# A windowed-attention and Fourier-mixing stack: logits and probabilities kept as heads, rows, keys; channel-matrix splits and cell sums moved among the second tile's steps

## The chip, the cores and the metric

The kernel runs on one core of one Trainium2 chip. A core has TensorE (PE in the profile; PEld is its weight load), VectorE (DVE), ScalarE (ACT), GpSimd (POOL) and SyncE (SP, which here issues nearly all transfers), and sixteen DMA engines between its on-chip memory (SBUF) and HBM. PE writes its results to a second on-chip memory, PSUM, in eight banks. The metric is the device time of one execution in microseconds, as a median over executions. Less is better.

## The reference

Four layers act on x of 2048 positions by 640 channels: attention, Fourier mixing, attention, Fourier mixing. Each adds its result to its input, and each normalises its input first.

```python
def _A_ref(x, wqkv, wo):            # H = 32 heads of Dh = 20, window W = 8, dilation 2
    q, k, v = ...                   # x @ wqkv
    idx = pos[:, None] - off[None, :]       # positions s, s-2, ..., s-14
    logits = jnp.einsum("bhsd,bhswd->bhsw", q, kg) * scale
    logits = jnp.where(mask, logits, -1e9)
    attn = _softmax(logits, axis=-1)
    o = jnp.einsum("bhsw,bhswd->bhsd", attn, vg)
    return o.reshape(B, S, D) @ wo
...
def _B_ref(x, dft_seq_re, dft_seq_im, dft_hid_re, dft_hid_im):
    a = jnp.einsum("bsd,ed->bse", x, dft_hid_re)
    b = jnp.einsum("bsd,ed->bse", x, dft_hid_im)
    return jnp.einsum("ts,bse->bte", dft_seq_re, a) - jnp.einsum("ts,bse->bte", dft_seq_im, b)
...
x = A_x
x = x + _A_ref(_layernorm(x), A_wqkv, A_wo)
x = x + _B_ref(_layernorm(x), ...)
x = x + _A_ref(_layernorm(x), A_wqkv, A_wo)
x = x + _B_ref(_layernorm(x), ...)
```

So every position attends to eight keys in each head, and each Fourier layer is a real part of a two-dimensional transform written as products with given matrices.

## The kernel before

**Precision and data.** Matrices are multiplied in a reduced format, so each factor is split into a high and a low part: ACT writes the high part, DVE (or POOL) subtracts it from the source and writes the low part, and PE makes three products (`PASSES`, L215). Positions are permuted on the host, even ones first, so that the dilated window becomes eight neighbouring rows. A chunk `c` is 512 positions: 128 partitions of four rows `j`.

**Attention (`layer_a`, L239).** A plan of steps is written out by hand: `at(step, phase, fn)` records work, and the loop at L816 replays it in the order of steps and, in a step, of `PHASES` (L808), so the order on all five engines is fixed (L812). A unit `u` is one chunk and four heads (`HE`), in two halves `jp` of two rows; unit u has steps 2u and 2u+1, and there are 32 units a layer. For a half:

- `qk_mul` (L425) multiplies queries by the keys' window on DVE into `pr`, as rows, keys, heads, channels; POOL adds the ten upper channels of each head to the ten lower ones (L430).
- `qk_red` (L433) sums the ten remaining channels on DVE into the logits `lg`, 64 results for a half. `lg` is laid out as rows, keys, heads: `[P, NJ, W, HE]`.
- `soft` (L446) acts on a whole unit, 128 logits a partition: the mask (L451), the maximum over keys (L453), its subtraction (L455), the sum (L457) after ACT's exponential, the reciprocal (L459), and the product (L461), which writes the probabilities to a bank of PSUM that stays allocated (`pq`). `mx` and `sm`, 16 values each, lie in the same bank as rows, heads.
- `av_mul` (L464) multiplies the window of values by each probability, repeated over 20 channels; POOL adds the eight keys in three instructions (`av_tree`, L474).

The products with the weights (L359), with the output matrix (L506) and, late in the layer, the first output tile of the next Fourier layer (`z_mm`, L907) are put between these steps.

**Fourier mixing (`LayerB`, L845).** The sequence transform comes first, for eight tiles of 256 output positions: a tile is 16 steps over the 2048 input positions, and a step is fifteen matmuls into five banks (`z_mm`). The result is copied and split out of the banks (`evac`, L980, through `zt_put`, L960) and multiplied with the channel matrices (`ymm`, L985), whose result is added to the layer's input and stored (`yout`, L1004; the additions are L1009). Tiles 0 and 1 are made so; the other six go in three pairs by a scheme with seven products in place of eight (`pair`, L1093), which needs sums and differences of blocks of the input (cells): `x_whole` (L1036) adds high and low parts, `x_combine` (L1043) makes one combination (L1049), splits it in a buffer `stg` of which there are two (L1050, L1051), and stores it to HBM (L1052). `load_w` (L926) loads and splits the two channel matrices, five pieces each, through a ring of two buffers `xa`; the splits are L128 on ACT, L132 and L130 on DVE.

`run` (L1229) puts this together: the evacuation of tile 0, all of `load_w`, then sixteen steps of tile 1, with the first output block's `ymm` and `yout` behind step 3, two fifths of the second block's `ymm` behind step 13, and three items of cell work behind each step from step 2 on. In `run` only PE's order is fixed by hand (L1236); the order on the other engines comes from the compiler's own scheduler. All of them work in order, SP's queue of transfers too.

Of the kernel before, what the change touches and what calls it, by code (L numbers as in the profile page):

```python
# [36 lines left out]
LEAD0 = (-7, -6, -5, -4, -3, -2, -1, 0, 1, 1, 2, 3, 3, 4, 5, 5)  # L37


THIN = ((20, 24, 26, 28, 32, 36, 40, 44), (12, 16, 20, 24, 28, 32, 36, 44, 48))  # L40
OUTP = (((20, 24, 28, 32), (36, 40, 44, 46)), ((20, 24, 28, 32), (36, 40, 44, 46)))
LNS = ((40, 52), (40, 52))


LEAD2 = (-7, -6, -5, -4, -2, 0, 0, 1, 1, 2, 3, 4, 4, 6, 6, 7)
ZTHIRDS = (
# [4 lines left out]
)  # L51
# [3 lines left out]
NWIN = 5  # L55
# [19 lines left out]
def tile_layers(ctx: ExitStack, tc: tile.TileContext, x, wqkv, wo, cs, wre, wim, out):  # L75
# [21 lines left out]
    nc.vector.memset(warm, 0.0)  # L97
    nc.scalar.activation(warm, warm, AF.Exp)
    T([P, 8], "pad0")
# [34 lines left out]
    class Stats:  # L134
        def __init__(self):
# [30 lines left out]
        def var_eps(self, j):  # L166
            nc.scalar.activation(self.rstd[:, j : j + 1], self.var[:, j : j + 1], AF.Copy, bias=EPS, scale=1.0 / D)  # L167

        def finish(self, j0=0, j1=4):
            r = self.rstd[:, j0:j1]  # L170
# [19 lines left out]
    def load_x(src, j, tag="xa"):  # L190
        xt = T([P, D], tag, bufs={"xa": 2}.get(tag, 1))
# [47 lines left out]
    def layer_a(li, stats, handoff, prev):  # L239
        xin, xout = xs[li], xs[li + 1]  # L240
        first = li == 0
        ly = li // 2
        nstats = [None] * NC
# [7 lines left out]
        win = {}  # L251
        lgs = {}
# [18 lines left out]
        def x_stats(c, j, fast=False):  # L271
            if j == 0:
                stats[c] = Stats()
# [88 lines left out]
        def qkv_evac(g, cqj):  # L362
            c, q, j = cqj
            if j % 2 == 0:
                sgs[q] = T([P, 6, 2, FE], "stg", bufs=2)
# [21 lines left out]
        def q_load(u):  # L387
            c, e = u // NE, half(u, 0)[0]
            src = qb[c][e // 2]
            qs[u] = T([P, NJ, FE], "qs")  # L390
# [34 lines left out]
        def qk_mul(u, jp):  # L425
# [4 lines left out]
            nc.gpsimd.tensor_tensor(pv[:, :, 0:10], pv[:, :, 0:10], pv[:, :, 10:20], op=ALU.add)  # L430
            prq[(u, jp)] = pv

        def qk_red(u, jp):  # L433
            if jp == 0:
                lgs[u] = T([P, NJ, W, HE], "lg", bufs=2)
            nc.vector.tensor_reduce(  # L436
                lgs[u][:, 2 * jp : 2 * jp + 2].rearrange("p j w h -> p (j w h)"),
                prq.pop((u, jp))[:, :, 0:10],
# [7 lines left out]
        def soft(u, part):  # L446
            lg = lgs[u]
            v = nc.vector
            if part == 0 and (u // NE) % 2 == 0:
                mw = bass.AP(tensor=mk.tensor, offset=mk.offset, ap=[mk.ap[0], [1, NJ], [1, W], [0, HE]])  # L450
                v.tensor_tensor(lg, lg, mw, op=ALU.add)  # L451
            if part == 1:
                v.tensor_reduce(mx, lg.rearrange("p j w h -> p j h w"), axis=AX.X, op=ALU.max)  # L453
            if part == 2:
                v.tensor_tensor(lg, lg, mx.unsqueeze(2).to_broadcast([P, NJ, W, HE]), op=ALU.subtract)  # L455
            if part == 3:
                v.tensor_reduce(sm, lg.rearrange("p j w h -> p j h w"), axis=AX.X, op=ALU.add)  # L457
            if part == 4:
                v.reciprocal(sm, sm)  # L459
            if part == 5:  # L460
                v.tensor_tensor(pp, lg, sm.unsqueeze(2).to_broadcast([P, NJ, W, HE]), op=ALU.mult)  # L461
                lgs[u] = pp

        def av_mul(u, jp):  # L464
            pr = prod()
            nc.vector.tensor_tensor(  # L466
                pr.rearrange("p j w (h d) -> p j w h d", d=DH),
                lgs[u][:, 2 * jp : 2 * jp + 2].unsqueeze(4).to_broadcast([P, 2, W, HE, DH]),
                wview(u, jp, 1, [[DH, HE], [1, DH]]),
# [44 lines left out]
        def wo_add(c, j, e0=0, e1=2):  # L514
            for e in range(e0, e1):
                if e == 0 and j == 0:
                    nstats[c] = Stats()
# [27 lines left out]
        def wq_split(q, k):  # L545
            split(wq[q][:, 0, k], wq[q][:, 1, k], wq[(q, k)], eng=nc.gpsimd if k % 2 else None)
# [23 lines left out]
        def early():  # L570
# [8 lines left out]
            def xt(j, part):  # L579
# [3 lines left out]

            prev.pair(
                NPAIR - 1,
                stats,
                {
# [731 lines left out]
```

## Time and profile before

| | before |
|---|---|
| median of three runs | 1804.51 us |
| lowest, highest | 1800.17, 1807.22 us |
| the profiled execution | 1801.87 us |
| span of its instructions | 1800.0 us |
| mean granted PE clock | 0.991 |
| first attention layer | up to about 400 us |
| second attention layer | about 930 to 1290 us |
| DMA, moved | 423.59 MB, mean 235 GB/s |

A profile is of one execution, and its busy times are shares of an average over stages with different limits. A group of instructions is given by source line, engine, operation, the tiles written and read, and shapes, with busy time, mean nanoseconds of one, and what ended the idle time ahead of it. The chain of waits is followed back from the last instruction, at each step to what released it; a piece of another engine in it says that this engine's time passes on to the end. A filter by stretch gives each engine's busy microseconds and, in brackets, its instructions.

### The profile page before, as it was taken

Reading aid. Unit: us, or ns where it says so; the run is one execution under the profiler, and the core shown is the slowest. Engines: PE = TensorE matmul, PEld = TensorE weight load, DVE = VectorE, ACT = ScalarE, POOL = GpSimd, SP = SyncE. Lnnn points to the kernel's source line nnn. Section 1 sums busy time; section 2 is a strip of 40 time slices with the busy share of each in tenths; the row PEclk is TensorE's granted clock in tenths of the full one; section 3 lists DMA queues with packets and bytes.
Section 4 is the critical chain, followed back from the end, with each engine's and each line's share of the span. In section 5 each row is a group of like instructions: output and inputs, shape, how many; then the busy total and the mean of one; then the engine's idle time right before and its main releaser. Section 6 shows DMA issues by size and latency. Waiting matters only on the chain.

```text
span 1800.0 us, 26493 instructions
## 1 busy us (share of the span) xinstructions
PE 1735.3 (96%) x8798; PEld 1506.4 (84%) x8798; DVE 1391.0 (77%) x2135; ACT 818.6 (45%) x1708; POOL 633.5 (35%) x591
## 2 busy tenths in 40 slices
PE   9999997989999999999999999998899999999999
PEld 6889896877788888888888899987787888888888
DVE  5899899987767767768739988899777676677673
ACT  5544644544445445445533334444434443443441
POOL 3799898960000000000008987889400000000000
PEclk9999999999999999999999999999999999999999
DMA  6776667648787887888737856687687876876861
GB/s 232 225 264 205 212 206 250 216 147 293 255 264 256 284 271 251 290 270 268 246 124 223 284 183 199 201 300 260 218 283 258 265 237 219 267 230 228 265 211 53
DMA packets 273994, 423.59 MB, mean 235 GB/s; under 512 B 22688, under 2 KB 153248, under 8 KB 273600
## 3 DMA queue, kind: packets, MB, share of 16 engines
q1 hardware_dynamic: 270656, 419.92, 71.7%
q10 hardware_dynamic: 3200, 1.97, 0.4%
q8 instruction: 70, 1.15, 0.3%
q14 instruction: 68, 0.56, 0.1%
HBM read 336.66 MB, written 85.14 MB: 234 GB/s over the span
## 4 chain that ended last, share of the span: by engine, by line
PE 63%; DVE 14%; DMA 11%; POOL 6%; ACT 3%; issue 2%; SPq 0%; DVEq 0%; ACTq 0%; POOLq 0%
PE m L359 16%; PE aux L996 12%; PE t L1085 9%; PE m L1085 9%; PE pq L1085 5%; PE xt L1085 4%; DMA xc<-stg 4%; PE aux L506 4%; DVE pr L428 2%; DMA win<-cs_in 2%; DVE pr L466 2%; POOL pr L481 2%; POOL pr L430 1%; POOL r L868 1%; DMA xa<-cs_in 1%
## 5 line engine op out<-in xcount | busy, mean ns | idle before, releaser
L359 PE MATMUL m<-r,s 128*128 128x480 f32 x1920 | 438.9, 383 | 6.2 <-ACT s L229 3.8
L359 PEld LDWEIGHTS m<-r,s 128*128 128x128 f32 x1920 | 358.1, 190 | 60.8 <-ACT s L229 5.5
L1078 ACT CAST r<-win 128x512 fp32r<-128x512 f32 x251 | 152.9, 620 | 175.3 <-DVE win L1114 86.9
L171 POOL TENSOR_TENSOR stats<-stats,mhalf 128x1 f32<-128x1 f32 (+1 forms) x40 | 29.1, 727 | 565.8 <-ACT stats L167 565.7
L996 PE MATMUL aux<-r2a,zo 128*128 128x320 f32 x768 | 226.0, 309 | 0.0
L481 POOL TENSOR_TENSOR pr<-pr 128x640 f32<-128x640 f32 x126 | 204.5, 1623 | 41.9 <-DVE pr L466 41.5
L428 DVE TENSOR_TENSOR pr<-pq,win 128x1280 f32<-128x1280 f32 x128 | 189.8, 1483 | 26.9 <-ACT pq L401 24.6
L996 PE MATMUL aux<-pr,zo 128*128 128x320 f32 x704 | 207.8, 309 | 0.0
L1079 DVE TENSOR_TENSOR r<-win,r 128x512 fp32r<-128x512 f32 x251 | 168.9, 687 | 45.7 <-ACT r L1078 43.5
L466 DVE TENSOR_TENSOR pr<-pq,win 128x1280 f32<-128x1280 f32 x128 | 190.8, 1491 | 4.5 <-DVE pq L461 0.2
L430 POOL TENSOR_TENSOR pr<-pr 128x640 f32<-128x640 f32 x128 | 183.5, 1434 | 19.8 <-DVE pr L428 17.0
L1085 PE MATMUL m<-r,r 128*128 128x512 f32 x594 | 151.7, 390 | 0.8 <-DVE r L1079 0.5
L996 PEld LDWEIGHTS aux<-r2a,zo 128*128 128x128 f32 x768 | 144.1, 188 | 1.9
L918 PE MATMUL m<-s,r 128*128 128x512 f32 x384 | 120.3, 401 | 18.1 <-DMA s<-c0b 7.1
L996 PEld LDWEIGHTS aux<-pr,zo 128*128 128x128 f32 x704 | 132.2, 188 | 2.0
L1085 PE MATMUL t<-r,r 128*128 128x512 f32 x495 | 132.6, 390 | 0.0
L1085 PEld LDWEIGHTS m<-r,r 128*128 128x128 f32 x594 | 111.2, 188 | 24.8 <-DVE r L1079 1.1
L918 PE MATMUL t<-s,r 128*128 128x512 f32 x384 | 117.4, 394 | 2.4 <-DVE ot L978 2.4
L482 POOL TENSOR_TENSOR pr<-pr 128x320 f32<-128x320 f32 x126 | 114.5, 909 | 9.9
L366 ACT COPY stg<-m 128x480 f32<-128x480 f32 x128 | 70.9, 556 | 100.4 <-PE m L359 88.1
L436 DVE TENSOR_REDUCE lg<-pr 128x64 f32<-128x640 f32 x128 | 104.0, 813 | 11.2 <-POOL pr L430 11.1
L1085 PEld LDWEIGHTS t<-r,r 128*128 128x128 f32 x495 | 92.9, 188 | 19.9
(270 smaller groups left out, 3231.8 us busy)
## 6 DMA issues: line engine op xcount, KB each, us to landing
win<-cs_in SPq DMA_DIRECT2D x358, 256.0 KB, 4.3
r<-xc SPq DMA_DIRECT2D x240, 256.0 KB, 4.5
win<-kvb SPq DMA_DIRECT2D x96, 440.0 KB, 4.7
xa<-cs_in SPq DMA_DIRECT2D x124, 256.0 KB, 4.3
win<-kvb SPq DMA_DIRECT2D x64, 360.0 KB, 5.1
xc<-stg SPq DMA_DIRECT2D x40, 512.0 KB, 3.7
kvb<-stg SPq DMA_DIRECT2D x60, 320.0 KB, 3.9
xr<-xs SPq DMA_DIRECT2D x40, 320.0 KB, 3.2
```

Of the source, the lines that this page charges most:

```text
L359: nc.tensor.matmul(mt[g][:, : 3 * F], st[:, a, k], wq[q][:, b, k], start=n == 0, stop=n == 14)
L428: nc.vector.tensor_tensor(pr, q, wview(u, jp, 0, [[1, FE]]), op=ALU.mult)
L430: nc.gpsimd.tensor_tensor(pv[:, :, 0:10], pv[:, :, 0:10], pv[:, :, 10:20], op=ALU.add)
L436: nc.vector.tensor_reduce(lgs[u][:, 2 * jp : 2 * jp + 2].rearrange("p j w h -> p (j w h)"), prq.pop((u, jp))[:, :, 0:10], axis=AX.X, op=AL ...
L466: nc.vector.tensor_tensor(pr.rearrange("p j w (h d) -> p j w h d", d=DH), lgs[u][:, 2 * jp : 2 * jp + 2].unsqueeze(4).to_broadcast([P, 2, ...
L481: g.tensor_tensor(pr[:, :, 0:4], pr[:, :, 0:4], pr[:, :, 4:8], op=ALU.add)
L482: g.tensor_tensor(pr[:, :, 0:2], pr[:, :, 0:2], pr[:, :, 2:4], op=ALU.add)
L918: self.last = nc.tensor.matmul(self.z[t][k], self.xn[c][:, a, j, k * P : (k + 1) * P], self.ct[s][:, b], start=s == 0 and i == 0, stop=s = ...
L996: self.last = nc.tensor.matmul(self.ym[e][:, :320], zt[(k, a, ri)][:, j2 * P : (j2 + 1) * P], w[:, e * 320 : (e + 1) * 320], start=(k, a, ...
L1078: nc.scalar.copy(hi, raw)
L1079: nc.vector.tensor_tensor(lo, raw, hi.bitcast(F32), op=ALU.subtract)
L1085: nc.tensor.matmul(bank, w(a, kb), hl[b], start=start and (a, b) == (0, 0), stop=stop and (a, b) == (1, 0),)
```

## The change

**Layout.** The logits become heads, rows, keys (`[P, HE, NJ, W]`), and so do the probabilities; `mx` and `sm` become heads, rows. The maximum and the sum then read eight neighbouring words for each result. `qk_red` goes through the same products in the same order and writes its results 32 words apart over heads; `av_mul` reads the probabilities with the same steps.

**Fourier layers.** `load_w` makes one piece a call, and its ten calls stand ahead of the cell work in one list, from which a number of items is taken behind each step of tile 1: none behind step 0, four behind steps 1 to 3, three behind each later one. The first block's `ymm` and `yout` move from behind step 3 to behind step 6.

**The rest.** A spare tile of eight words becomes a one-word constant that is set on DVE; the activation table is loaded by name (set 6 for set 0), once as before. All hand-written tables move into one, `CFG`, and generated lists are written out with the values that they had; options for other ways to finish the statistics (`ln`) and to sum without POOL (`whole`) are added and not used. The built order of PE, DVE, ACT, POOL and SP is the same outside the two stretches of `run`, but for the constant's memset.

```diff
+CFG = {
...
+ 'run': [{'pre': [0, 0, 0, 0, 0, 0, 0, 0, 0, 0, 0, 0, 0, 0, 0, 0],
+          'post': [0, 4, 4, 4, 3, 3, 3, 3, 3, 3, 3, 3, 3, 3, 3, 3],
+          'y': [[6, 6, 6, 6, 6], [13, 13, 16, 16, 16]]},
...
+    eps = T([P, 1], "eps")
+    nc.vector.memset(eps, EPS)
+    nc.scalar.add_instruction(
+        mybir.InstLoadActFuncSet(name=nc.get_next_instruction_name(), ins=[], outs=[], act_func_set_id=6)
+    )
     nc.scalar.activation(warm, warm, AF.Exp)
-    T([P, 8], "pad0")
...
+        def rows(lg, jp):
+            return lg[:, :, 2 * jp : 2 * jp + 2].rearrange("p h j w -> p (j w) h")
...
         def qk_red(u, jp):
             if jp == 0:
-                lgs[u] = T([P, NJ, W, HE], "lg", bufs=2)
+                lgs[u] = T([P, HE, NJ, W], "lg", bufs=2)
+            pv = prq.pop((u, jp))[:, :, 0 : 20 if (u, jp) in whole else 10]
             nc.vector.tensor_reduce(
-                lgs[u][:, 2 * jp : 2 * jp + 2].rearrange("p j w h -> p (j w h)"),
-                prq.pop((u, jp))[:, :, 0:10],
+                rows(lgs[u], jp),
+                pv.rearrange("p (a h) d -> p a h d", h=HE),
                 axis=AX.X,
                 op=ALU.add,
             )
...
-                mw = bass.AP(tensor=mk.tensor, offset=mk.offset, ap=[mk.ap[0], [1, NJ], [1, W], [0, HE]])
+                mw = bass.AP(tensor=mk.tensor, offset=mk.offset, ap=[mk.ap[0], [0, HE], [1, NJ], [1, W]])
                 v.tensor_tensor(lg, lg, mw, op=ALU.add)
             if part == 1:
-                v.tensor_reduce(mx, lg.rearrange("p j w h -> p j h w"), axis=AX.X, op=ALU.max)
+                v.tensor_reduce(mx, lg, axis=AX.X, op=ALU.max)
             if part == 2:
-                v.tensor_tensor(lg, lg, mx.unsqueeze(2).to_broadcast([P, NJ, W, HE]), op=ALU.subtract)
+                v.tensor_tensor(lg, lg, mx.unsqueeze(3).to_broadcast([P, HE, NJ, W]), op=ALU.subtract)
             if part == 3:
-                v.tensor_reduce(sm, lg.rearrange("p j w h -> p j h w"), axis=AX.X, op=ALU.add)
+                v.tensor_reduce(sm, lg, axis=AX.X, op=ALU.add)
...
             if part == 5:
-                v.tensor_tensor(pp, lg, sm.unsqueeze(2).to_broadcast([P, NJ, W, HE]), op=ALU.mult)
+                v.tensor_tensor(pp, lg, sm.unsqueeze(3).to_broadcast([P, HE, NJ, W]), op=ALU.mult)
...
             nc.vector.tensor_tensor(
-                pr.rearrange("p j w (h d) -> p j w h d", d=DH),
-                lgs[u][:, 2 * jp : 2 * jp + 2].unsqueeze(4).to_broadcast([P, 2, W, HE, DH]),
-                wview(u, jp, 1, [[DH, HE], [1, DH]]),
+                pr.rearrange("p j w (h d) -> p (j w) h d", d=DH),
+                rows(lgs[u], jp).unsqueeze(3).to_broadcast([P, 2 * W, HE, DH]),
+                wview(u, jp, 1, [[1, FE]]).rearrange("p j w (h d) -> p j w h d", d=DH),
                 op=ALU.mult,
             )
...
-        pp = pq[:, NJ * FE : NJ * FE + NJ * W * HE].rearrange("p (j w h) -> p j w h", j=NJ, w=W)
+        pp = pq[:, NJ * FE : NJ * FE + NJ * W * HE].rearrange("p (h j w) -> p h j w", j=NJ, w=W)
...
-        def load_w(self):
-            self.wr = T([P, 2, KD, D], "r2a", F32R)
-            self.wi = []
-            for k in range(KD):
-                raw = load_x(wre, k)
-                split(self.wr[:, 0, k], self.wr[:, 1, k], raw)
-                raw = load_x(wim, k)
...
-                split(hl[0], hl[1], raw, neg=True)
-                self.wi.append(hl)
+        def load_w(self, i):
+            k = i // 2
+            if i == 0:
+                self.wr = T([P, 2, KD, D], "r2a", F32R)
+                self.wi = []
+            if i % 2 == 0:
+                split(self.wr[:, 0, k], self.wr[:, 1, k], load_x(wre, k))
+            else:
+                wt = T([P, 2, D], f"pr{k}" if k < 4 else "zo3", F32R)
+                split(wt[:, 0], wt[:, 1], load_x(wim, k), neg=True)
+                self.wi.append((wt[:, 0], wt[:, 1]))
...
         def run(self, nstats):
+            R = CFG["run"][self.li // 2]
             self.evac(0)
-            self.load_w()
             todo = []
             for i in range(0, NP, 2):
                 todo += [(self.x_whole, (side, i)) for side in (2, 0)]
                 todo += [(self.x_combine, (m, i)) for m in XC]
+            todo = [(self.load_w, (i,)) for i in range(2 * KD)] + todo
             with tc.manual_schedule(engines={nc.tensor.engine}):
                 for s in range(NST):
+                    for _ in range(R["pre"][s]):
+                        fn, args = todo.pop(0)
+                        fn(*args)
                     self.zpart(1, s, s + 1)
-                    if s == 3:
-                        self.ymm(0, 0, 0, KD)
-                        self.yout(0, 0, nstats)
-                    if s == 13:
-                        self.ymm(0, 1, 0, 2)
-                    if s > 1:
-                        for fn, args in todo[:3]:
+                    for h in range(2):
+                        ks = [k for k in range(KD) if R["y"][h][k] == s]
+                        if ks:
+                            self.ymm(0, h, ks[0], ks[-1] + 1)
+                        if 4 in ks:
+                            self.yout(0, h, nstats)
+                    for _ in range(R["post"][s]):
+                        if todo:
+                            fn, args = todo.pop(0)
                             fn(*args)
-                        todo = todo[3:]
```

In the built program the new order in the first of these stretches is, on DVE, around the first output block's additions (L1009): the tile splits of steps 6, 7 and 8, five combines and one whole sum come ahead of them that stood behind them or beside them before; and at its end the additions for the pair's fourth cell (L1114) come behind the evacuation of tile 1 and the last combine within it. The second Fourier layer has the same order there.

More of the change, by code (lines that the diff above doesn't have):

```diff
@@ L251, in layer_a @@
         win = {}
+        whole = {divmod(x, 2) for x in C["whole"]}
         lgs = {}
@@ L763, in layer_a @@
         for c, w, xtags in (
[L764 to L765 removed]
+            (2, C["w2"], None),
+            (3, C["w3"], ("xa", "xa")),
         ):
@@ L815, in layer_a @@
             nc.vector.tensor_copy(mk, mask)
-            for s in range(LEAD0[0], last + 1):
-                for ph in PHASES:
+            for s in range(gs[0], last + 1):
+                for ph in C["ph"][s >= 48].split():
                     for fn, args in plan.pop((s, ph), ()):
@@ L1173, in pair @@
                     self.product(f1, self.x_plain(*k2(i), 512), p21, False, i == NP - 1)
-                es = store("stg", 2)
+                es = store("stg", CFG["bufs"]["stg"])
                 for b in range(2):
```

219 lines of the change are left out of this document (125 added, 94 removed), and 13 rows, old and new, of tables (CFG, ZTHIRDS).

## The prediction

> **What bounds the kernel now.** I read the page first, then the engines' busy time by stretches, then the groups on VectorE, then the chain of waits.
>
> ```profile
> span 1800.0 us, 26493 instructions
> ...
> PE 1735.3 (96%) x8798; PEld 1506.4 (84%) x8798; DVE 1391.0 (77%) x2135; ACT 818.6 (45%) x1708; POOL 633.5 (35%) x591
> ...
> PE 63%; DVE 14%; DMA 11%; POOL 6%; ACT 3%; issue 2%; SPq 0%; DVEq 0%; ACTq 0%; POOLq 0%
> ```
>
> TensorE is busy for 96% of the span: only 64.7 us can be won without removing matmuls. The stretches (columns: PE, PEld, DVE, ACT, POOL busy) tell where they lie:
>
> ```profile
> 75.00:119.00 44.00, 39.32 (x171) 32.73 (x170) 42.68 (x54) 19.45 (x46) 37.16 (x34) 0.92 0.81 265
> 119.00:219.00 100.00, 99.98 (x527) 89.17 (x526) 90.56 (x127) 55.76 (x147) 91.05 (x88) 1.00 0.68 209
> 219.00:390.00 171.00, 152.32 (x796) 132.92 (x795) 158.28 (x229) 79.53 (x192) 158.95 (x142) 0.96 0.68 217
> 938.00:991.00 53.00, 51.49 (x247) 44.47 (x246) 47.78 (x64) 19.72 (x45) 42.43 (x39) 1.00 0.74 226
> 1157.00:1268.00 111.00, 101.96 (x547) 90.29 (x545) 99.68 (x152) 50.40 (x126) 100.62 (x92) 0.97 0.78 261
> 1450.00:1500.00 50.00, 50.00 (x260) 44.03 (x259) 36.19 (x62) 19.72 (x35) 0.00 (x0) 1.00 0.65 206
> ```
>
> The attention layers change bound. From 119 to 219 us PE has no gap, though DVE is 91% busy: a shorter DVE instruction is worth nothing there. From 75 to 119 DVE is the full engine (97%); from 219 to 390 and 1157 to 1268 DVE and POOL are both above 89% and PE waits. The Fourier layers are PE's, as 1450 to 1500 shows.
>
> **The change, part one: the layout.** The order of every engine's instructions in the two attention layers is the same in both built programs; only access patterns differ. These are the groups concerned (mean ns behind the busy time):
>
> ```profile
> L466 DVE TENSOR_TENSOR pr<-pq,win 128x1280 f32<-128x1280 f32 x128 | 190.8, 1491 | 4.5 <-DVE pq L461 0.2
> L428 DVE TENSOR_TENSOR pr<-pq,win 128x1280 f32<-128x1280 f32 x128 | 189.8, 1483 | 26.9 <-ACT pq L401 24.6 <-DMA win<-kvb 1.9 <-ACT stg L366 0.3
> L436 DVE TENSOR_REDUCE lg<-pr 128x64 f32<-128x640 f32 x128 | 104.0, 813 | 11.2 <-POOL pr L430 11.1
> L457 DVE TENSOR_REDUCE pq<-lg 128x16 f32<-128x128 f32 x64 | 25.1, 392 | 10.5 <-ACT lg L444 4.6
> L453 DVE TENSOR_REDUCE pq<-lg 128x16 f32<-128x128 f32 x64 | 25.1, 392 | 2.2
> L461 DVE TENSOR_TENSOR pq<-lg,pq 128x128 f32<-128x128 f32 x64 | 18.9, 296 | 2.2
> L455 DVE TENSOR_TENSOR lg<-lg,pq 128x128 f32<-128x128 f32 x64 | 17.8, 277 | 0.1
> L459 DVE RECIPROCAL pq<-pq 128x16 f32<-128x16 f32 x64 | 16.5, 258 | 0.1
> ```
>
> The maximum (L453) and the sum (L457) read 128 elements, each four words from the one before, in 392 ns. L455 and L461 pass over as many elements in 277 and 296 ns; their difference, 19 ns, is a result in PSUM. So about 96 ns of a reduction (392 - 296) look like the price of the stride, and with the keys side by side it goes. Bounds: 0, if the extra belongs to a reduction with 16 results in PSUM (L459 takes 258 ns for only 16 elements, which speaks for that), and 115 (392 - 277). I take 96, by the row with equal elements and an equal destination. That is 128 x 96 ns = 12.3 us of DVE time, but only what lies on the path counts. The chain of waits holds 18 pieces of L453 and 15 of L457, first and last of each:
>
> ```profile
> 77.08 0.40 DVE pq L453
> 1248.88 0.41 DVE pq L453
> ...
> 82.82 0.39 DVE pq L457
> 1253.30 0.40 DVE pq L457
> ```
>
> 33 x 96 ns = 3.2 us; the rest is behind PE or POOL. The upper bound lets every unit in the four stretches that PE does not fill have both savings. Filtered to L428, these stretches hold:
>
> ```profile
> sum 379.00, DVE 100.85; mean DVE 25.21
> ```
>
> 100.85 of 189.8 us, or 68 of 128 products, so 34 units: 34 x 2 x 115 ns = 7.8 us. I take 3.2.
>
> What the layout may cost: the reduction over channels (L436) now writes its 64 results 32 words apart, and the weighting product (L466) steps 32 words after every 20 repeats of a probability. No row shows either. L428 also jumps back in its PSUM operand, 16 times, and is not slower than L466 (1483 against 1491), and L436 writes one result for ten elements read, so I take 0. The upper bound is the strided read's 115/128 = 0.9 ns for each of 64 jumps, 58 ns an instruction. The subtraction, the mask's addition and the final product stay contiguous on their large operand; their broadcasts repeat one word, as L466's does already: 0.
>
> The Trainium skill (Vector Engine (DVE) Microarchitecture Reference, section 5.2, Measured stream behaviour on trn2) speaks against the new writes: a destination that hops at every element is given 1.71 to 2.51 ns a column against 1.054. If 64 results counted as columns, an estimate from that page is 42 to 93 ns more for each L436, which would take back most of the saving; no run shows it yet.
>
> A memset of one word and a named activation table, loaded once as before, come at the start, where PE waits for the first loads: 0.
>
> **Part two: the Fourier layers' start.** In both, PE multiplies tile 1 in steps of fifteen matmuls while DVE and ACT also split the ten channel-matrix pieces and make twenty combines of cell sums. First one such step, from one product into the third bank to the fourth after it (3.4 us); then PE's stalls in question; then DVE's queue before the second of these:
>
> ```profile
> 416.40 0.40 PE L918 MATMUL xt<-s,r 128*128 128x512 f32 x1
> 419.82 0.39 PE L918 MATMUL xt<-s,r 128*128 128x512 f32 x1
> ...
> 434.42 0.42 PE L996 MATMUL aux<-zo,ot 128*128 128x320 f32 x1 [0.31 <-DVE zo L130]
> 490.79 0.93 PE L1085 MATMUL t<-r 128*128 128x512 f32 x3 [1.91 <-DVE ot L978]
> ...
> 1324.70 0.42 PE L996 MATMUL aux<-zo,ot 128*128 128x320 f32 x1 [0.65 <-DVE zo L130]
> 1381.12 0.94 PE L1085 MATMUL t<-r 128*128 128x512 f32 x3 [1.83 <-DVE ot L978]
> ...
> 478.86 0.69 DVE L1049 TENSOR_TENSOR stg<-s,s 128x512 f32<-128x512 f32 x1 [0.51 <-DMA xc<-stg]
> 480.89 0.68 DVE L1049 TENSOR_TENSOR stg<-s 128x512 f32<-128x512 f32 x1
> 489.21 0.69 DVE L1114 TENSOR_TENSOR win<-xa,win 128x512 f32<-128x512 f32 x1 [1.51 <-DMA xa<-cs_in]
> 490.56 0.68 DVE L975 TENSOR_TENSOR ot<-t,ot 128x512 fp32r<-128x512 f32 x1
> ```
>
> The first output product waited 0.31 and 0.65 us for the last matrix piece. Three tile steps (10 us) later that piece has long been split (in DVE's queue it nearly keeps its place), so 0.96 us go. The scheduler had most splits and sums between the steps already, so "behind the first steps" moves few instructions on DVE, and none of evac(0). The two additions of the first output block (L1009) now stand nine instructions later and wait for a product that ends three steps later; the combines behind them, SP's stores of these, and the loads queued on SP behind the stores wait with them. Tile splits for the three steps come ahead of them, so PE is fed.
>
> The larger stall, 1.91 and 1.83 us: evac(1)'s last two pieces stood behind an L1114 that waited 1.51 us for a transfer PE needs only three cells later. In the new order that addition comes after the evacuation; instead, the last combine (before at 480.89) moves into it, with five other instructions between it and the combine ahead. From that one's start, 478.86, a run without waits of 0.6 to 0.7 us each puts the last combine at about 483, and ten shorter instructions behind it end at 488.2, not at 491.2. PE would get there at 488.9 less the 0.3 already won: I take 0.5 us a layer as left, so 0.96 + 3.74 - 1.0 = 3.7 us. Bounds: 4.7 (nothing left), and a loss by the ring below.
>
> **Sum.** The profiled execution took 1801.87 us, 1.87 around its span: 1801.87 - 3.2 - 3.7 = 1795.0. The median of the three runs shown is 1804.51, 2.6 more than this execution; I keep the sum on its own base and leave that spread to the range.
>
> **The rivals.** (a) More of it: the 34 units all shorten (34 x 192 ns = 6.5) and the stalls go whole: 1801.87 - 6.5 - 4.7 = 1790.7. For it: DVE at 97% from 75 to 119. Against it: POOL at 93% from 219 to 390 takes over after little.
>
> (b) The layout does nothing, since 392 ns belongs to the form: 1801.87 - 3.7 = 1798.2. L459 speaks for it, L436 against (813 ns for 640 elements leaves no large fixed part).
>
> (c) The scattered results cost 58 ns: 33 of 68 reductions were on the chain, so as many L436 would add 33 x 58 ns = 1.9: 1796.9. The skill's rule on destinations would be this case.
>
> (d) Slower: the ring of staging buffers. The chain runs through their stores, from
>
> ```profile
> 415.58 0.35 DVE stg L1049
> ...
> 419.43 5.45 DMA xc<-stg
> ...
> 474.61 4.23 DMA xc<-stg
> ```
>
> in the first Fourier layer: twenty combines share two buffers, 65.3 us from the first (415.58) to the last (480.89), 3.4 us each. If the late additions hold the ring, evac(1), which now contains the last combine, is held too. Up to 485.6 (483 + 2.6) for that combine PE loses no more than before; from there each microsecond costs two, one a layer. It outweighs parts one and the matrix pieces (4.2) beyond 487.7. Three combines late (493) is 2 x 7.4 - 4.2 = 10.6 slower: 1812.5. Against it: the first combines keep their places, and so does nearly every store on SP.
>
> **How the numbers follow.** Chances: forecast 0.44, (a) 0.22, (b) 0.14, (c) 0.08, (d) 0.12. About 0.5%, 9 us, is what a measurement of this kernel can tell from no change; from 1804.51, faster means below 1795.5. That takes a little over half of the forecast, nearly all of (a) and little else: 0.48. Slower means above 1813.5, the bad end of (d) and of unknown prices: 0.10. The rest, 0.42, is the same. The range goes from (a) with the upper price and some run spread, 1785, to (d)'s end, 1813.
>
> **What would show it.** The new L453 and L457 lines at about 296 ns (b: still 392), L436 at 813 and L466 at 1491 (c: L436 near 870); DVE near 1379 us; no stall of 1.9 us before the first t products; the twentieth combine near 483. It is wrong if DVE's time falls and the attention layers end when they did (POOL took over), or if combines start later and PE waits at evac(1).

## The result, and the profile after

| | before | after |
|---|---|---|
| median, nine runs each | 1804.51 us | 1797.37 us |
| lowest, highest | 1800.17, 1807.82 us | 1794.46, 1799.55 us |
| the profiled execution | 1801.87 us | 1798.85 us |

The ratio of after to before is 0.9962 with a 95% interval of [0.9949, 0.9974]: 7.1 us less, between 4.7 and 9.2. The two profiled executions are only 3.0 us apart, because that of before was one of its quicker ones and that of after one of its slower ones. The spans alone can't size the change; single stretches of several traces, and timed runs of its parts, can.

The page of after, its span, its busy times and the engines' shares of the chain of waits:

```profile
span 1797.1 us, 26504 instructions
...
PE 1737.8 (97%) x8798; PEld 1508.5 (84%) x8798; DVE 1375.7 (77%) x2136; ACT 818.1 (46%) x1708; POOL 633.3 (35%) x591
...
PE 67%; DVE 11%; DMA 9%; POOL 7%; ACT 3%; issue 2%; SPq 0%; ACTq 0%; DVEq 0%; POOLq 0%
```

DVE is busy for 15.3 us less (before 1391.0), 12.5 of them in the maximum and the sum. Of the chain it has 11% in place of 14%, and POOL 7% in place of 6%. The groups concerned (lines have moved: L528 and L532 are the old L453 and L457, L511 is L436, L541 is L466, L498 is L428):

```profile
L498 DVE TENSOR_TENSOR pr<-pq,win 128x1280 f32<-128x1280 f32 x128 | 189.7, 1483 | 28.7 <-ACT pq L471 26.3 <-DMA win<-kvb 2.2
...
L541 DVE TENSOR_TENSOR pr<-pq,win 128x1280 f32<-128x1280 f32 x128 | 190.9, 1491 | 4.3
...
L511 DVE TENSOR_REDUCE lg<-pr 128x64 f32<-128x640 f32 x128 | 104.2, 814 | 18.0 <-POOL pr L501 17.8
...
L532 DVE TENSOR_REDUCE pq<-lg 128x16 f32<-128x128 f32 x64 | 18.8, 294 | 11.2 <-ACT lg L519 5.5
L528 DVE TENSOR_REDUCE pq<-lg 128x16 f32<-128x128 f32 x64 | 18.9, 295 | 2.2
```

The maximum and the sum take 295 and 294 ns in place of 392. The reduction over channels, whose results now lie 32 words apart, takes 814 ns (813 before), and the product that steps through the probabilities 1491, as before. So the layout has no price. L511 waits 17.8 us for POOL's sums where L436 waited 11.1: part of the time won on DVE turned into that wait. In the stretches of the attention layers (PE, PEld, DVE, ACT, POOL busy):

```profile
75.00:119.00 44.00, 40.84 (x181) 34.32 (x180) 42.45 (x56) 20.75 (x49) 38.95 (x35) 0.92 0.83 272
219.00:390.00 171.00, 155.21 (x803) 136.06 (x803) 153.95 (x227) 78.94 (x191) 157.87 (x141) 0.95 0.67 214
1157.00:1268.00 111.00, 101.44 (x543) 89.41 (x541) 96.89 (x152) 50.83 (x128) 100.25 (x92) 0.97 0.79 262
```

From 75 to 119 PE does 1.5 us more work than before in the same time, from 219 to 390 2.9 us more; from 1157 to 1268 it has no more. In the Fourier layers' starts no first product waits for a matrix piece any more, but the other stall is there still. PE's rows, then DVE's queue ahead of the first of them:

```profile
488.43 0.93 PE L1132 MATMUL t<-r 128*128 128x512 f32 x3 [1.63 <-DVE ot L1025]
...
1378.22 0.94 PE L1132 MATMUL t<-r 128*128 128x512 f32 x3 [1.63 <-DVE ot L1025]
```

```profile
478.04 0.69 DVE L1096 TENSOR_TENSOR stg<-s,s 128x512 f32<-128x512 f32 x1 [1.20 <-DMA xc<-stg]
...
483.68 0.68 DVE L1096 TENSOR_TENSOR stg<-s 128x512 f32<-128x512 f32 x1
...
487.87 0.41 DVE L1025 TENSOR_TENSOR ot<-t,zo 128x256 fp32r<-128x256 f32 x1
488.20 0.68 DVE L1022 TENSOR_TENSOR ot<-t,ot 128x512 fp32r<-128x512 f32 x1
...
490.46 0.69 DVE L1161 TENSOR_TENSOR win<-xa,win 128x512 f32<-128x512 f32 x1 [0.25 <-DMA xa<-cs_in]
```

The addition that waits for a transfer (L1161, before L1114) stands behind the evacuation, as foreseen. The last combine starts at 483.68 (forecast: about 483), and the tenth instruction behind it (L1022) ends at 488.20 + 0.68 = 488.88 (forecast: 488.2). PE waits for the ninth, which ends at 487.87 + 0.41 = 488.28, and PE was there at 488.43 - 1.63 = 486.80, not at 488.6. These times look near the forecast's, but the stretch as a whole began earlier: tile 0's evacuation (its first L1025) starts at 406.04, where it started at 410.45 before. Counted from there, the last combine comes 77.6 us later, not 70.4 as before.

### The profile page after: what moved, and what is told of

The parts are those of the page before. It is cut to its first block, busy times and chain, and to the rows that moved or that the text cites. A ratio compares the mean times of both kernels' runs of the same rounds, so it can differ in the third digit from the quotient of the medians.

```text
span 1797.1 us, 26504 instructions
## 1 busy us (share of the span) xinstructions
PE 1737.8 (97%) x8798; PEld 1508.5 (84%) x8798; DVE 1375.7 (77%) x2136; ACT 818.1 (46%) x1708; POOL 633.3 (35%) x591
## 4 chain that ended last, share of the span: by engine, by line
PE 67%; DVE 11%; DMA 9%; POOL 7%; ACT 3%; issue 2%; SPq 0%; ACTq 0%; DVEq 0%; POOLq 0%
PE m L429 18%; PE aux L1043 12%; PE t L1132 9%; PE m L1132 9%; PE pq L1132 5%; PE xt L1132 5%; PE aux L581 4%; DMA win<-cs_in 3%; DMA xc<-stg 2%; POOL pr L556 2%; DVE pr L498 2%; POOL pr L501 2%; DVE pr L541 2%; POOL r L919 1%; PE t L969 1%
## 5 line engine op out<-in xcount | busy, mean ns | idle before, releaser
L556 POOL TENSOR_TENSOR pr<-pr 128x640 f32<-128x640 f32 x126 | 204.2, 1621 | 36.6 <-DVE pr L541 36.0
L498 DVE TENSOR_TENSOR pr<-pq,win 128x1280 f32<-128x1280 f32 x128 | 189.7, 1483 | 28.7 <-ACT pq L471 26.3
L541 DVE TENSOR_TENSOR pr<-pq,win 128x1280 f32<-128x1280 f32 x128 | 190.9, 1491 | 4.3
L436 ACT COPY stg<-m 128x480 f32<-128x480 f32 x128 | 71.1, 556 | 115.9 <-PE m L429 100.8
L511 DVE TENSOR_REDUCE lg<-pr 128x64 f32<-128x640 f32 x128 | 104.2, 814 | 18.0 <-POOL pr L501 17.8
```

The costliest lines, as they stand in the source:

```text
L498: nc.vector.tensor_tensor(pr, q, wview(u, jp, 0, [[1, FE]]), op=ALU.mult)
L511: nc.vector.tensor_reduce(rows(lgs[u], jp), pv.rearrange("p (a h) d -> p a h d", h=HE), axis=AX.X, op=ALU.add,)
L541: nc.vector.tensor_tensor(pr.rearrange("p j w (h d) -> p (j w) h d", d=DH), rows(lgs[u], jp).unsqueeze(3).to_broadcast([P, 2 * W, HE, DH]) ...
L556: g.tensor_tensor(pr[:, :, 0:4], pr[:, :, 0:4], pr[:, :, 4:8], op=ALU.add)
```

## The experiments

All ratios are to the kernel before, from five rounds each unless said otherwise; 0.001 is 1.8 us.

| run | layout | order of `run` | `stg` buffers | ratio, 95% interval |
|---|---|---|---|---|
| after | new | new | 2 | 0.9962 [0.9949, 0.9974] |
| e1_layout | new | old | 2 | 0.9974 [0.9964, 0.9985] |
| e2_run | old | new | 2 | 0.9979 [0.9966, 0.9992] |
| e12_only_ymm_ring2 | new | only first block moved | 2 | 0.9961 [0.9947, 0.9975] |
| e3_ring3 | new | new | 3 | 0.9936 [0.9924, 0.9948] |
| e11_ring4 | new | new | 4 | 0.9938 [0.9924, 0.9951] |
| e5_old_order_ring3 | new | old | 3 | 1.0016 [1.0003, 1.0028] |
| e9_only_ymm | new | only first block moved | 3 | 0.9925 [0.9912, 0.9938] |
| e10_only_list | new | only the one list | 3 | 1.0022 [1.0012, 1.0032] |
| e4_nomax | new, no maximum | new | 2 | 0.9921 [0.9904, 0.9937] |
| e6_nomax_ring3 | new, no maximum | new | 3 | 0.9864 [0.9844, 0.9883] |
| e7_whole | as e6, less POOL work | new | 3 | 0.9854 [0.9836, 0.9872] |

**Each part alone.** e1_layout is the changed kernel with the old order:

```diff
- 'pre': [0, 0, ...], 'post': [0, 4, 4, 4, 3, ...], 'y': [[6, 6, 6, 6, 6], ...]
+ 'pre': [10, 0, ...], 'post': [0, 0, 3, 3, 3, ...], 'y': [[3, 3, 3, 3, 3], ...]
```

> Part one alone (the new layout, the old order of the Fourier layers' start). By the prediction's sum it gives 3.2 of the 6.9 us: ratio to before about 0.9982. Rival, from the two traces (the profiled attention layers end 2.9 and about 0 us earlier, and POOL pieces on the chain of waits rose in their place): POOL takes over and it gives under 2 us, above 0.999. Second rival: the layout is nearly all of the measured 7.1 us, because each microsecond won in an attention layer is kept: 0.9965 or less.

e2_run has the new order, and `lg`, the probabilities, `mx` and `sm` as in the kernel before:

```diff
-                lgs[u] = T([P, HE, NJ, W], "lg", bufs=2)
+                lgs[u] = T([P, NJ, W, HE], "lg", bufs=2)
...
-                v.tensor_reduce(mx, lg, axis=AX.X, op=ALU.max)
+                v.tensor_reduce(mx, lg.rearrange("p j w h -> p j h w"), axis=AX.X, op=ALU.max)
```

> Part two alone (the new order of the Fourier layers' start, the old layout). By the prediction's sum 3.7 us: ratio about 0.998, with no stall above 0.5 us ahead of the first output products of the first pair. Rival, from the trace of after, where that stall is still 1.6 and about 1.5 us because combines and evacuation are paced by the ring of two staging buffers: only the 0.96 us of the matrix pieces and the small rest, 1 to 2 us in all, 0.999 to 0.9995, with a stall of 1.5 to 1.9 us still there.

The layout gave 4.7 us [2.7, 6.5], the order 3.8 [1.4, 6.1]. Neither part is idle, and both forecasts, 3.2 and 3.7, lie inside. The order's own share can be had a second way, after against e1_layout: 0.0012, or 2.2 us, with an uncertainty of 2.9. The rivals of 0.9965 for the layout and 0.999 for the order lie just inside the intervals, so the times don't exclude them. The trace of e2_run decides against the forecast's mechanism for the order, since the stall is still there:

```profile
491.80 0.93 PE L1132 MATMUL t<-r 128*128 128x512 f32 x3 [1.66 <-DVE ot L1025]
...
1380.46 0.93 PE L1132 MATMUL t<-r 128*128 128x512 f32 x3 [1.13 <-DVE ot L1025]
```

The traces size the parts more sharply. From the first product with keys to the last weighting product of the first attention layer it is 387.12 - 34.04 = 353.1 us before and 354.5 in e2_run, but 349.9 to 350.5 in the eight traces that have the new layout and the maximum: 3.6 us less. The same stretch of the second layer has 337.2 and 339.8 against 334.7 to 338.4, in the mean 2.2 us less with a spread as large. From the first to the last L1025 of the two evacuations (tile 0, then tile 1), the two Fourier layers have 79.8 and 79.8 us before, and 79.7 and 79.6 in e1_layout; in the four traces with the first block moved and two buffers the means are 79.7 and 78.3. So the traces have the layout at more than 3.2 and the order at less than 3.7.

**Why more than 3.2.** About 1.4 us of the first layer come from one instruction that the change doesn't touch. DVE's and POOL's rows at that place, in the kernel before:

```profile
100.89 1.54 POOL L481 TENSOR_TENSOR pr<-pr 128x640 f32<-128x640 f32 x1
100.92 2.20 DVE L560 TENSOR_TENSOR r2a<-zo,r2a 128x640 fp32r<-128x640 f32 x1
```

and after:

```profile
100.60 0.82 DVE L635 TENSOR_TENSOR r2a<-zo,r2a 128x640 fp32r<-128x640 f32 x1
...
100.67 2.18 POOL L556 TENSOR_TENSOR pr<-pr 128x640 f32<-128x640 f32 x1
```

Both have their operands in SBUF alone. Before, POOL's addition began 0.03 us ahead, and DVE's split took 2.20 us; after, with DVE 0.3 us earlier, the split came first by 0.07 us, took 0.82, and POOL's addition took 2.18. It is the first way in both traces with the old layout, and the second in all eight that have the new layout and the maximum. The chain of waits of the kernel before holds this piece:

```profile
101.00 2.11 DVE r2a L560
```

DVE has no slack there (42.68 of 44 us busy), and the time is kept: the weighting product ahead of this place starts 0.3 us sooner than before (99.00 against 99.32), the next one behind it 1.8 us sooner (104.47 against 106.27), and the last of the layer 3.0 us (384.10 against 387.12). By the Trainium skill (SBUF — State Buffer, the section "SBUF: two separate sides") such a pair of instructions shares one port pair, which goes whole to the one that starts first; the rows agree. Beyond that, 4.7 - 1.4 = 3.3 us are left for 12.4 us of shorter reductions (128 x 97 ns), or 27%, and the forecast's share was 33 of 128; by the interval it is 1.3 to 5.1 us.

**The ring of staging buffers.** Between the evacuations of the two tiles lie the twenty combines, which share the buffers `stg`. In the traces, for the first and the second Fourier layer:

| run | layout, order, buffers | twentieth combine behind the first L1025 of tile 0, us | PE's wait ahead of the first `t` product, us |
|---|---|---|---|
| before | old, old, 2 | 70.4, 70.6 | 1.91, 1.83 |
| e1_layout | new, old, 2 | 70.6, 70.2 | 1.74, 1.75 |
| e2_run | old, new, 2 | 75.3, 73.6 | 1.66, 1.13 |
| after | new, new, 2 | 77.6, 74.2 | 1.63, 1.63 |
| e3_ring3 | new, new, 3 | 57.8, 58.5 | 0, 0 |

With the old order the combines keep their pace under either layout. In e1_layout tile 0 is evacuated 3.6 us sooner than before (406.90 against 410.45), the twentieth combine comes 3.4 us sooner (477.49 against 480.89), and the `t` product 3.6 us sooner (487.19 against 490.79), so the time won in the attention layer passes through the ring whole. (Later in this trace most of it is gone: the second attention layer's first product comes 0.3 us sooner, at 938.35 against 938.64. Which waits took it was not followed up.) It is the new order that puts the combines 3 to 7 us later when they have two buffers. In the trace of after they also hold up the splits for tile 1 itself, which go through the same queues. In DVE's, ACT's and PE's rows:

```profile
457.67 0.69 DVE L1096 TENSOR_TENSOR stg<-s,s 128x512 f32<-128x512 f32 x1 [2.66 <-DMA xc<-stg]
...
458.44 0.62 ACT L1097 CAST stg<-stg 128x512 fp32r<-128x512 f32 x1 [4.23 <-DVE stg L1096]
458.97 0.61 ACT L941 CAST s<-win 128x512 fp32r<-128x512 f32 x1
...
459.63 0.74 PE L969 MATMUL m<-s,r 128*128 128x512 f32 x2 [0.97 <-ACT s L941]
```

A combine waits for a store out of the ring, its copy on ACT waits for the combine, a tile split stands behind that copy, and PE waits for the split. At 465.79 PE waits 1.04 us more for such a split; before, there was one wait of this kind, of 0.42 us, in each layer. e3_ring3 gives the combines a third buffer:

```diff
- 'bufs': {'xa': 2, 'qs': 1, 'stg': 2, 'xr': 1},
+ 'bufs': {'xa': 2, 'qs': 1, 'stg': 3, 'xr': 1},
```

> The changed kernel with three staging buffers in place of two. If the ring paces the twenty combines and so the evacuation behind them, the waits of combines for stores (13.1 us in the first stretch) fall below 4 us, the twentieth combine starts 3 us or more before 483.7, the stall of 1.6 us ahead of the first pair goes in both layers, and the kernel is about 3 us faster than the changed one: 0.9945 against before. Rival: the stores land at the pace of SP's queue and the transfers, so a third buffer moves the wait and changes nothing: 0.996.

0.9936, as the first theory had it: 0.0026 or 4.7 us less than after, with an uncertainty of 3.1. Its evacuation of tile 0 starts at 406.95, and then, in DVE's and PE's rows:

```profile
464.79 0.68 DVE L1096 TENSOR_TENSOR stg<-s 128x512 f32<-128x512 f32 x1
...
482.48 0.42 DVE L1025 TENSOR_TENSOR ot<-t,zo 128x256 fp32r<-128x256 f32 x1
...
483.18 0.87 PE L1132 MATMUL t<-r 128*128 128x512 f32 x3
```

The twentieth combine comes 57.8 us behind the evacuation, not 77.6, and the product starts without a wait, in the second layer too; the waits for tile splits are gone as well (none above 0.25 us). So in the new order two buffers paced that stretch. A fourth buffer (e11_ring4) adds nothing:

> The changed kernel with four staging buffers. With three, combines still wait 3.4 and 2.8 us for stores in the two stretches, but no stall of PE hangs on them any more: 0.9936 as with three. Rival: combines further ahead take VectorE and the transfers from the tile's own steps, 1 us or more slower than three, 0.9942 or more; or the last waits still counted, 0.993 or less.

0.9938. Three are enough.

**What the new order is for.** With three buffers the old order is not merely as good or a little worse:

> The new layout and three staging buffers, with the old order of the Fourier layers' start. If the new order is worth something of its own (the matrix pieces' stall, and the late L1161 addition behind the evacuation), it is 1 to 3 us slower than the same kernel in the new order: 0.9945 to 0.995 against before. Rival: the ring alone set the end of that stretch, and with three buffers the old order is as good: 0.9936.

1.0016, 14 us slower than e3_ring3, far past what either theory expected, and 7.6 us slower than the same order with two buffers (e1_layout). PE's rows:

```profile
437.35 0.63 PE L1043 MATMUL aux<-zo,ot 128*128 128x320 f32 x1 [6.38 <-ACT zo L188]
...
1332.87 0.64 PE L1043 MATMUL aux<-zo,ot 128*128 128x320 f32 x1 [5.69 <-ACT zo L188]
```

and DVE's and ACT's rows ahead of the first:

```profile
431.99 0.69 DVE L1096 TENSOR_TENSOR stg<-s 128x512 f32<-128x512 f32 x1 [1.09 <-DMA xc<-stg]
432.76 0.62 ACT L1097 CAST stg<-stg 128x512 fp32r<-128x512 f32 x1 [2.81 <-DVE stg L1096]
...
435.27 0.69 DVE L1096 TENSOR_TENSOR stg<-s,s 128x512 f32<-128x512 f32 x1 [1.17 <-DMA xc<-stg]
436.04 0.62 ACT L1097 CAST stg<-stg 128x512 fp32r<-128x512 f32 x1 [2.67 <-DVE stg L1096]
436.56 0.73 ACT L188 ACTIVATE zo<-xa 128x640 fp32r<-128x640 f32 x1
```

On ACT the last split (L188) stands behind the copies of eight combines, where it stands behind five with two buffers; the last two are shown. They wait for DVE, and DVE's combines for a store out of the ring (1.09 and 1.17 us). The waits, 12.1 us in the two layers, are not all of the loss: the granted clock is 0.57 from 434 to 442 us and 0.53 from 1329 to 1340, where e3_ring3 has 1.00 in the same steps (429 to 437, 1316 to 1327). The two things in the new order, the move of the first block and the one list, were then tried one at a time: e9_only_ymm has `y` at step 6 with the ten splits ahead of step 0, e10_only_list has `y` at step 3 and `post` as new, but four items behind step 0 too.

> New layout, three staging buffers, and of the new order of the Fourier layers' start only the move of the first output block from behind step 3 to behind step 6 (the matrix splits stand ahead of the steps as of old). If the 14 us between the old and the new order with three buffers are the first product's wait for the last matrix piece (6.4 and 5.7 us in the two layers' traces), the move alone brings nearly all of it back: 0.9936 to 0.995 against before, and no wait above 1 us at that piece. Rival: the place of the splits in the list matters too (combines get ahead of the splits on VectorE and ScalarE as long as these stand in another list), 0.997 or more.

> New layout, three staging buffers, and of the new order only the one list with the ten splits ahead of the cell work, four items behind each of the steps 0 to 3; the first output block stays behind step 3. By the first theory of the run beside it, PE still waits 3 us or more for the last matrix piece in each layer: 1.000 or a little less against before. By the rival the wait goes with the list, 0.9936 to 0.995.

The move alone has 0.9925, like e3_ring3, the list alone 1.0022, like e5_old_order_ring3, with waits of 5.77 and 6.37 us. So by these times the move is the whole of part two, and the list does nothing that can be measured. With two buffers:

> New layout, the two staging buffers of old, and of the new order only the move of the first output block. With three buffers the move did all and the list nothing. If that holds with two, this is the changed kernel's time, 0.9962 against before, and the twentieth combine starts 74 to 78 us after the evacuation of the tile before, as in the changed kernel (70.5 in the old order). Rival: with two buffers the list's order matters, since the additions at the end of the stretch stand otherwise: the evacuation's stall is 1.9 us as before and the time that of the layout alone, 0.9974, with the twentieth combine at 70.5 us.

0.9961, the changed kernel's time, with the twentieth combine 74.1 and 74.7 us behind the evacuation. So it is the move, too, that puts the combines 4 us later than in the old order (70.4) when they have two buffers. Which transfer or wait in the ring does this was not settled.

**What a microsecond of DVE is worth.** e4_nomax leaves out the maximum and its subtraction:

```diff
-            if part == 1:
-                v.tensor_reduce(mx, lg, axis=AX.X, op=ALU.max)
-            if part == 2:
-                v.tensor_tensor(lg, lg, mx.unsqueeze(3).to_broadcast([P, HE, NJ, W]), op=ALU.subtract)
```

> The changed kernel without the maximum and its subtraction ahead of the exponential (the softmax is computed from unshifted logits): 128 VectorE instructions fewer, 64 x (295 + 277) ns = 36.6 us of its time, six times what the layout's 96 ns a reduction saved on them. If a saving on VectorE is worth the share of pieces that lies on the chain of waits (about a quarter, 24 to 33 of 128), 8 to 10 us come off: 0.991 against before. Rival, POOL is the co-bound and takes over at once: under 3 us, 0.9945 or more.

0.9921; against after (0.9921 / 0.9962) 7.4 us less for 36.6 us of DVE, 20%, with an uncertainty of 4 us. That is above the rival's 3 us, and a quarter, 9.2 us, lies inside. So the share of pieces on the chain is not contradicted as a price for DVE's time. With three buffers (e6_nomax_ring3):

> The changed kernel without the maximum and its subtraction, and with three staging buffers. The two savings lie in different layers; if they add, 0.9936 x 0.9921 / 0.9962 = 0.9895 against before (19 us). Rival: the time won in an attention layer is lost at the next ring or transfer, 0.992.

0.9864: the two savings at least add (0.9895 was expected, itself uncertain by 0.0025). Against e3_ring3 the same 36.6 us are worth 13.0 us here, 36%, again with an uncertainty of 4 us. e7_whole also takes nine POOL additions a layer away:

```diff
-         'whole': [],
+         'whole': [27, 31, 35, 39, 43, 47, 51, 55, 59],
```

> As the run without the maximum and with three staging buffers, and in nine of the 64 halves of each attention layer VectorE sums all twenty channels itself, so that POOL loses nine additions of 1.43 us (12.9 us a layer) and VectorE's nine reductions read 1280 elements in place of 640 (about 0.7 us each, 6.1 us a layer). If POOL is the co-bound of the late stretches, each is worth about half of that to the path: 4 to 8 us less in all, 0.985 to 0.987. Rival: VectorE is the bound there, and it is slower by up to 6 us, 0.993.

0.9854, 1.8 us below e6_nomax_ring3 with an uncertainty of 4.8 us: whether the exchange is worth anything stays open, and only the rival's 6 us slower is excluded. The pages (busy times of e6_nomax_ring3, then of e7_whole) show the exchange, 24.0 us off POOL for 11.5 on DVE:

```profile
PE 1730.5 (97%) x8798; PEld 1504.5 (85%) x8798; DVE 1339.8 (75%) x2008; ACT 818.7 (46%) x1708; POOL 632.5 (36%) x591
```

```profile
PE 1729.4 (97%) x8798; PEld 1504.7 (85%) x8798; DVE 1351.3 (76%) x2008; ACT 818.0 (46%) x1708; POOL 608.5 (34%) x573
```

**Versions that beat both.** Without touching what is computed, e9_only_ymm and e3_ring3 (0.9925 and 0.9936). e7_whole at 0.9854 (1778.41 us) is the quickest tried; it rests on logits small enough for an exponential without the maximum.

**The price of a step.** e8_probe, made for its rows and not for its time, puts these ahead of the first layer, four times each:

```diff
+        nc.vector.tensor_reduce(pc[:, 0:16], pa[:, 0:128].rearrange("p (g w) -> p g w", w=8), ...)
+        ... "p (g w s) -> p g s w", w=8, s=2
+        ... "p (g w s) -> p g s w", w=8, s=4
+        ... "p (w s) -> p s w", w=8
+        nc.vector.tensor_reduce(pb[:, 0:64], pa[:, 0:128].rearrange("p (g w) -> p g w", w=2), ...)
+        nc.vector.tensor_reduce(pb[:, 0:128].rearrange("p (h g) -> p g h", h=4)[:, 0:16], ...)
+        nc.vector.tensor_tensor(pb[:, 0:512], pa[:, 0:512], pa[:, 512:1024], op=ALU.add)
+        nc.vector.tensor_tensor(pb[:, 0:512].rearrange("p (h g) -> p g h", h=4), ...)
```

> The changed kernel with eight forms of VectorE instruction, four of each, ahead of the first layer, in which the cost of a step is seen by itself: reductions of 128 elements to 16 with the elements of a result 1, 2, 4 and 16 words apart; reductions of 128 elements to 64 with results side by side, and 32 words apart; an addition of 512 elements to neighbouring words, and to words 128 apart. If the stride of 4 words cost the 97 ns, strides of 4 and 16 take 97 ns or more over stride 1 and stride 2 lies between; if a scattered result costs only where one comes in each cycle, the two reductions to 64 take the same and the two additions differ by 300 ns or more. Rival: a scattered result never costs anything, or costs 1 to 2 ns each wherever it stands (64 to 128 ns in the second pair).

The four strides are L168, L169, L172 and L175, then L176 and L177, L180 and L181; by groups of lines (busy us and mean ns behind the bar):

```profile
L181 DVE TENSOR_TENSOR pr<-pr 128x512 f32<-128x512 f32 x4 | 4.1, 1032 | 0.0
L180 DVE TENSOR_TENSOR pr<-pr 128x512 f32<-128x512 f32 x4 | 2.7, 683 | 0.0
...
L172 DVE TENSOR_REDUCE pq<-pr 128x16 f32<-128x128 f32 x4 | 1.5, 376 | 0.0
L175 DVE TENSOR_REDUCE pq<-pr 128x16 f32<-128x128 f32 x4 | 1.5, 369 | 0.0
L169 DVE TENSOR_REDUCE pq<-pr 128x16 f32<-128x128 f32 x4 | 1.1, 284 | 0.0
L176 DVE TENSOR_REDUCE pr<-pr 128x64 f32<-128x128 f32 x4 | 1.1, 282 | 0.0
...
L177 DVE TENSOR_REDUCE pr<-pr 128x64 f32<-128x128 f32 x4 | 1.1, 279 | 0.0
L168 DVE TENSOR_REDUCE pq<-pr 128x16 f32<-128x128 f32 x4 | 1.1, 266 | 0.0
```

Steps of 4 and 16 words cost 110 and 103 ns for 128 elements, a step of 2 words 18 or less (the first L168, behind a memset, took 0.23 us, the other three 0.27 to 0.28). Results 32 words apart cost nothing with one for two elements (282 and 279), but 349 ns in an addition that writes one for each (683, 1032). The rival is refuted. The addition's results lie 128 words apart, so the length of the step is not told apart from how often a result comes.

## Why the prediction was right, and where it was not

The forecast was 1795.0 on the base of the profiled execution, 6.9 us of gain; 7.1 was measured between the medians, which makes the time 2.4 us longer than the figure, the spread that the sum had left to the range. The median is not below 1795.5, to which the larger chance (0.48) had been given, but in the part that had 0.42. That the two gains agree to 0.2 us is in part luck, as the terms show.

- **The bound** was read rightly, as far as the times can tell: 12.4 us of DVE time gave about 3.3 (forecast 3.2, interval 1.3 to 5.1), and L511's waits for POOL rose by 6.7 us. Rival (a), in which all 34 units shorten and the stalls go whole, is a gain of 11.2 us, outside the interval, and the stalls did not go.
- **The price of the stride**, 96 ns by L461's row: 97 and 98. Rival (b) is refuted by that, and by the strides of the probe.
- **Scattered results at 0 ns**: 814 against 813, 1491 against 1491. Rival (c) is refuted for this form. The Trainium skill (Vector Engine (DVE) Microarchitecture Reference, section 5.2, Measured stream behaviour on trn2) gives 1.71 ns a column against 1.054 for a destination that hops at every element, 0.66 more; the addition agrees (349 ns for 512 elements, 0.68 each). The estimate of 42 to 93 ns, which counted the reduction's 64 results as such columns, does not hold: it measured 1 ns.
- **What the sum left out of part one**: the 1.4 us of L560. Its row was in the trace of before, 2.20 us beside others of 0.82, and in its chain of waits.
- **Part two was too large.** The matrix pieces' 0.96 us went, as forecast. The step that failed is the one that starts DVE's queue "from that one's start, 478.86": it left the nineteenth combine at its old time in the new order. So "I take 0.5 us a layer as left" came out at 1.63 in each, and 0.48 of 3.74 us were won there, not 2.7. e2_run, which has the new order alone, shows it in the first layer. PE reaches the stall at 491.80 - 1.66 = 490.14, 78.4 us behind the evacuation of tile 0 (411.73 there), as forecast (488.6 - 410.45 = 78.2). But the twentieth combine comes 75.3 us behind that evacuation, not 483 - 410.45 = 72.6. In the changed kernel 483.68 is near the forecast by luck: the stretch began 4.4 us sooner, mostly by part one (3.6 us in e1_layout), and the combine came 7.2 us later in it.
- **What the sum left out of part two**: "Tile splits for the three steps come ahead of them, so PE is fed" took no account of combines that wait ahead of a split. In the changed kernel's trace PE waits 0.97 and 1.04 us for splits, and from its first to its last L1025 the first Fourier layer takes 81.8 us, 2.0 more than before, the second 78.4, 1.4 less (the means of the four traces are 79.7 and 78.3).
- **Rival (d)** named this ring as the danger, and it was at work. Its point of decision, 485.6, is 75.2 us behind the evacuation of tile 0. The combine came behind that point in the changed kernel's first layer (77.6), which took longer, by its tile splits and not by the evacuation's stall, and ahead of it in the second (74.2). The large slowdown came only with three buffers in the old order, by way of the splits.

So the sum came out right through two terms that were off in opposite directions: part one by 1.5 us too small, part two by 1.5 to 2.3 too large. These are the runs' own estimates; each has an uncertainty of 2 to 3 us, and the traces point the same way.

## What to carry to other kernels

When a change moves work in a stretch that a ring of buffers paces, don't carry the ring's times over from the old trace. Count them from the start of the stretch, and ask what the new order puts ahead of each store: here twenty combines on two buffers took their last at 70 us in the old order and at 74 to 78 in the new one. Compare a forecast time inside a kernel in the same way, since a shift of the whole stretch can make a wrong forecast look right. A third buffer and a later consumer belong together: with the third, the new order won 4.7 us and the old one lost 7.6, since work that gets ahead of a split in an in-order queue delays whoever waits for the split. A saving on an engine that shares its bound with another is worth only a share of itself. The pieces on the chain of waits said a quarter here, and 20% and 36% were measured, each with an uncertainty of about 11 points.

## What the runs showed of the hardware

- Order at a tie decides: 0.1 us between the starts of a DVE and a POOL instruction on 640 elements, each with its operands in SBUF, made DVE's 1.4 us shorter and POOL's 0.6 us longer (2.20 and 1.54 us, or 0.82 and 2.18).
- A step of 2 words in a DVE reduction is nearly free (284 ns against 266) and one of 4 costs as much as one of 16 (376, 369): the price begins between them and then doesn't grow.
- Scattered results of a reduction, one for two elements and 32 words apart, cost nothing (279 ns against 282); those of an addition, one for each element and 128 words apart, 0.68 ns an element (349 / 512).
- Behind the waits of PE of 6.38 and 5.69 us in e5_old_order_ring3 the granted clock was 0.57 from 434 to 442 us and 0.53 from 1329 to 1340; around the stalls of 1.91 and 1.83 us in the kernel before it was 1.00.
